# More of attention's output projection behind its last scores, the mixer's first norm five steps sooner, and the last output projection in two halves

## The chip, the core and the metric

The kernel runs on one core of one Trainium2 chip. The metric is the device time of one execution in microseconds (us); the kernel before was run three times. Its engines are TensorE (PE; its weight loads are shown apart as PEld), VectorE (DVE), ScalarE (ACT), GpSimd (POOL) and SyncE (SP), which issues the transfers (DMA). A matmul reads an operand that was loaded into the array ahead of it and writes to one of the PSUM banks.

## The reference

Two layers are applied twice in turn to x of 2048 rows by 640 columns: attention with a memory (A) and a gated mixer (B).

```
x = x + A(layernorm(x));  x = x + B(layernorm(x))
x = x + A(layernorm(x));  x = x + B(layernorm(x))

A:  q, k, v = x @ wq, x @ wk, x @ wv         # 32 heads of 20; 4 segments s of 512 rows
    for s in range(4):                       # M, z: sums over earlier segments
        p = softmax(qs @ ks.T * scale + causal_mask)
        a_mem = phi(qs) @ M / (phi(qs) @ z + 1e-6)
        o_s = g * a_mem + (1 - g) * (p @ vs)
        M = M + phi(ks).T @ vs;  z = z + sum(phi(ks))
    return concat(o_s) @ wo

B:  z = gelu(x @ w_in)                       # 640 -> 1728
    z1, z2 = z[:, :864], layernorm(z[:, 864:])
    g = w_sp @ z2 + b_sp                     # w_sp is 2048 x 2048, over the rows
    return (z1 * g) @ w_out                  # 864 -> 640
```

## The kernel before

**Products in three parts.** An f32 operand is split into a high and a low f16 part, and a product is made of three matmuls: high by high, high by low, low by high. A projection of 640 to 320 columns is thus 5 x 3 = 15 matmuls in one bank. Rows are worked in 16 tiles of 128.

**Attention** (`Attention.run`) makes one list of 64 pairs: 4 segments by 16 pairs of heads. A pair has three steps, so the steps go from t = 0 to 191, with some steps of lead ahead and a few behind in which the last pairs are finished (`END`). In each step `scores` issues matmuls of queries by keys twice over: once for a pair several steps ahead, into mp, whose row maxima VectorE takes (mx, L1289), and once for the pair of the step, into es (L1273, masks L1245), of which ScalarE makes the exponentials P (L1282). `maxes` (L1307 to L1312) turns the maxima into a row (mr) and stores it beside the queries in qk with two small transfers on SP, one for its high and one for its low part; es needs both. `cast` splits P into PH (ScalarE, L1299) and PL (L1300: GpSimd, or VectorE for the second head of the last four pairs). `pvs` multiplies them with the values vs (L1326: 20 matmuls pv for a head, each with a load of PH or PL). `combine` scales the sums (ab on VectorE, L1342), adds them on GpSimd, and for each group of heads makes a high and a low part ohl (ScalarE L1353, GpSimd L1354) and stores the two parts with two transfers (L1357) to o in DRAM.

Between these steps stand the dense jobs: the projections to queries and keys (L1107), to values (v0 to v15, L1050), and the output projection of a tile, p0 to p11 (`project`: o is loaded by a transposing transfer at L1065, x at L1074; two halves of 15 matmuls yps, L1083; VectorE adds x at L1089; x1 is stored at L1091). The output of tiles 12 to 15 is projected in the mixer instead. `order` lists the jobs, and PACE says how much of them goes with a step from each time on, in units of work:

```
U, V = 6480, 4530
PACE = (-LEAD, 2400), (0, 700), (53, 1150), (128, 1250), (END + G, 0)
```

U is the work of one unit of queries and keys, V that of one projection. TensorE's order is the order of this code; the order of the other engines' instructions and of SP's queue is decided when the kernel is built, by a scheduler that knows priorities.

**The mixer's first product** (`phase1b`) takes tile after tile: load x1 (L275) or, for tiles 12 to 15, load o by a transposing transfer (L281) and x (L278) and project them; norm (xn, on VectorE, with two small GpSimd operations); cast to a high and a low part (xnhl, ScalarE L231); transpose by a transfer (th, L233); 30 matmuls zp by the second half of the weights (wi1), then 30 by the first half (wi0), all L316; gelu on ScalarE (L322). The first tile's norm may be issued ahead of attention's end: `self.first = self.ended()`, taken in `run` at step 3N - 4 = 188 of the 192, raises the priority of the first two loads, of the first norm and of its transpose, and lets them go behind the instructions that were the last on the engines at that step.

In the first round wi0 is read from the input in five pieces of 128 x 864 (`Weight.load`, L123, into wst, of which there are two buffers); each piece is split into a high part (wi0h, ScalarE L84) and a low part (wi0l, VectorE L85). In the second round the split halves are read back from DRAM.

**The spatial product and the output** are `phase2` in the first round and `phase2s` in the second. `phase2s` works on pairs of tiles, with seven products over blocks of w_sp in five banks a to e. `gate` multiplies by z1 and makes the operand ut; `tail` is the output projection of one tile (21 matmuls in each of two halves, cyp, L506; one addition of x1 on VectorE over both halves, xo, L509; one store, L510). The last two tiles' `tail` stand at the end, behind the loop over the pairs.

Of the kernel before, what the change touches and what calls it, by code (L numbers as in the profile page):

```python
# [9 lines left out]
F32 = mybir.dt.float32  # L10
# [5 lines left out]
ALU = mybir.AluOpType  # L16
# [382 lines left out]
def phase2s(g, w_sp, x1_d, z1_d, zb, w0, out):  # L399

    nc, tc = g.nc, g.tc
    KO, NP = 7, NT // 2
    RING = 6
    kn = [128] * 6 + [FH - 768]
    ks = [0, 1, 2, 3, 6, 7, 4, 5]
    with ExitStack() as ctx:
# [3 lines left out]
        po, pt1, pt0 = pool("do", 1, side="right"), pool("dtr1", 1, side="right"), pool("dtr0", 1, side="right")  # L410
# [67 lines left out]
        def fetch(nm, t, src):  # L478
            o = p2.tile([128, src.shape[-1]], F32, tag=nm, name="c" + nm)
            nc.sync.dma_start(o, src)  # L480
            return o
# [14 lines left out]
            nc.sync.dma_start(ut.rearrange("p l k c -> p (l k) c"), hl.rearrange("p l c -> p (l c)"), transpose=True)  # L496
            return t, ut[:, 0], ut[:, 1], xs

        def tail(t, uh, ul, xs, x1=None):
            if x1 is None:  # L500
                x1 = fetch("x1", t, x1_d[t])
            yp = py.tile([128, 2, 512], F32, tag="yp", name="cyp")
            for k in range(KO):
                for j, (a, b) in enumerate(((uh, woh), (uh, wol), (ul, woh))):
                    for n in range(2):
                        nc.tensor.matmul(yp[:, n, :320], a[:kn[k], k, :], b[:kn[k], k, n * 320:(n + 1) * 320],  # L506
                                         start=(k == 0 and j == 0), stop=(k == KO - 1 and j == 2))
            xo = po.tile([128, 2, 320], F32, tag="xo", name="xo")
            nc.vector.scalar_tensor_tensor(xo, yp[:, :, :320], xs, x1.rearrange("p (n c) -> p n c", n=2), ALU.mult, ALU.add)  # L509
            return lambda: nc.sync.dma_start(out[t], xo.rearrange("p n c -> p (n c)"))  # L510
# [27 lines left out]
        woh, wol = g.wu.place(w0)  # L538
        for _ in g.wu.load(None):
            pass  # L540
        pend, sent = [], lambda: None
        for p in range(NP):
            t, last = 2 * p, p + 1 == NP
            bank = lambda nm: pg.tile([128, 512], F32, tag=nm, name="g" + nm)
            vec = lambda nm: pv.tile([128, FHH], F32, tag=nm, name=nm)
            u, u1 = [p2.tile([128, FH], F32, tag="u", name="u") for _ in range(2)]
            pa, pb, pc, pd, pe = [bank(nm) for nm in "abcde"]
            v, v1, q, q1 = [vec(nm) for nm in ("v", "v1", "q", "q1")]
            n = 7 * p
# [22 lines left out]
            if pend:  # L572
                sent = tail(*pend.pop(0))
# [12 lines left out]
            x1 = [fetch("x1", i, x1_d[i]) for i in (t + 1, t)[:2 - last]] + [None]  # L586
# [18 lines left out]
            plus(u[:, FHH:], pe, t, u[:, FHH:])  # L605
            pend.append((*gate(t, u, z1[1]), x1[1]))
            sent = lambda: None
        for x in pend:
            tail(*x)()


def phase2(g, w_sp, x1_d, z1_d, zh, zl, out, nxt):
# [242 lines left out]
class Attention:  # L855
# [365 lines left out]
    def fetch(self, n):  # L1221

        assert n - self.NQK <= self.last, (n, self.last)
        assert NU * (n // 16) + min(n % 16 // 3, NU - 1) <= self.stacked, (n, self.stacked)
        for h in range(2):
            c = 40 * (n % 16) + 20 * h
            self.last_of["SP"] = self.nc.sync.dma_start(self.qk[n % self.NQK][64 * h:64 * h + 60], self.st[n // 16 % 2][c:c + 20].rearrange("p l i c -> (p l) i c")).ins
# [133 lines left out]
    def run(self, nseg=NSEG):  # L1361
        pairs = [(s, m, h0) for s in range(nseg) for m in range(NU) for h0 in UH[m][::2]]
        N = self.N = len(pairs)
        LEAD = self.LEAD = 3 * self.LM + self.LF
        G = 48
        END = 3 * N + self.LV + 3
# [9 lines left out]


        U, V = 6480, 4530
        PACE = (-LEAD, 2400), (0, 700), (53, 1150), (128, 1250), (END + G, 0)
        order = "02 03 v4 04 v5 v6 v7 10 11 12 13 14 v8 v9 v10 v11 20 21 p0 22 23 24 v12 v13 v14 v15 30 31 p1 32 p2 33 p3 34 p4 p5 p6 p7 p8 p9 p10 p11".split()  # L1380

        def step(w):

            for (t, p), (e, _) in zip(PACE, PACE[1:]):
                if w <= p * (e - t):
# [81 lines left out]
        def until(t):  # L1467
            while streams:
                e = min(streams)
                if e[0] >= t:  # L1470
                    return
                with self.hold() if e[1] < 2 else ExitStack():
                    e[0] = next(e[2], None)
                if e[0] is None:
                    streams.remove(e)
# [2 lines left out]
            self.later[3 * i - LEAD + 8] = [lambda w=w: self.update(*w)]  # L1478
        for t in range(-LEAD, END):
            self.now = t  # L1480
            if t == 3 * N - 4:
                self.first, self.end_of = self.ended(), [*self.last_of.values()]
            f, c = divmod(t + self.LF, 3)
            if c == 0 and 0 <= f + self.LM < N:
                self.fetch(f + self.LM)
            p, r = divmod(t - self.LV - 2, 3)
            if r == 0 and 0 <= p < N:
                self.combine(p, *pairs[p])
            n, c = divmod(t, 3)
            self.scores(n, c)  # L1490
            for f in self.later.pop(t, ()):
                f()
            for h in range(2):
                p, r = divmod(t - self.LV - h, 3)
                if r == 0 and 0 <= p < N:
                    for _ in self.pvs(p, h, *pairs[p]):
                        pass
                if h == 1 and c == 0 and 0 <= n - 1 + self.LM < N:
                    self.maxes(n - 1 + self.LM)
                if r == 0 and 0 <= p + 1 < N:  # L1500
                    self.cast(p + 1, h)
            until(t + 1)
# [87 lines left out]
```

## Time and profile before

| | |
|---|---|
| median of three runs | 2333.38 us |
| the runs | 2327.29, 2333.38, 2336.17 us |
| the profiled execution | 2329.32 us |
| its span in the trace | 2327.4 us |
| mean granted TensorE clock | 0.983 |
| busy: PE, PEld | 2172.4 us (93%), 1299.1 us (56%) |
| busy: DVE, ACT, POOL | 1502.1 us (65%), 1174.6 us (50%), 974.4 us (42%) |
| chain that ended last | PE 69%, DVE 9%, ACT 7%, DMA 6%, issue 3% |

All times below are us from the start of the span. A row of the timeline has the start, the duration, the engine (SPq: a transfer's issue on SyncE), the line, the operation, output <- input and the shape; xN stands for N instructions in a row, and a bracket for the idle time ahead of them and what ended it. Durations of many instructions are busy times. PE's share is that of an engine that has something in the array, which is not the same as full speed.

### The profile page before, as it was taken

Reading aid. Unit: us, or ns where it says so; the run is one execution under the profiler, and the core shown is the slowest. Engines: PE = TensorE matmul, PEld = TensorE weight load, DVE = VectorE, ACT = ScalarE, POOL = GpSimd, SP = SyncE. Lnnn points to the kernel's source line nnn. Section 1 sums busy time; section 2 is a strip of 40 time slices with the busy share of each in tenths; the row PEclk is TensorE's granted clock in tenths of the full one; section 3 lists DMA queues with packets and bytes.
Section 4 is the critical chain, followed back from the end, with each engine's and each line's share of the span. In section 5 each row is a group of like instructions: output and inputs, shape, how many; then the busy total and the mean of one; then the engine's idle time right before and its main releaser. Section 6 shows DMA issues by size and latency. Waiting matters only on the chain.

```text
span 2327.4 us, 50389 instructions
## 1 busy us (share of the span) xinstructions
PE 2172.4 (93%) x20490; PEld 1299.1 (56%) x20490; DVE 1502.1 (65%) x2790; ACT 1174.6 (50%) x1452; POOL 974.4 (42%) x726
## 2 busy tenths in 40 slices
PE   5878889899989999999999888999997999999998
PEld 2445455656645555555555555656665555555655
DVE  7678878876664544445335788787766767546454
ACT  3369678877742332122113887887775324322221
POOL 2168678988720000000001888888875323000000
PEclk9999899999999999999999999999998999999999
DMA  5653544545463458878645336453465433977875
GB/s 162 165 139 95 129 114 124 136 142 131 128 190 101 123 172 220 225 216 216 168 134 145 75 101 168 113 130 89 121 175 149 108 102 101 263 201 192 226 206 123
DMA packets 509417, 350.16 MB, mean 150 GB/s; under 512 B 409280, under 2 KB 444224, under 8 KB 504064
## 3 DMA queue, kind: packets, MB, share of 16 engines
q1 hardware_dynamic: 509184, 346.93, 56.1%
q8 instruction: 161, 2.64, 0.5%
q14 instruction: 72, 0.59, 0.1%
HBM read 160.83 MB, written 97.93 MB: 111 GB/s over the span
## 4 chain that ended last, share of the span: by engine, by line
PE 69%; DVE 9%; ACT 7%; DMA 6%; issue 3%; POOL 2%; SPq 1%; ACTq 0%; DVEq 0%; POOLq 0%
PE zp L316 15%; PE gp L668 12%; PE cyp L700 4%; PE pv L1326 4%; PE cyp L506 4%; PE yps L1083 3%; PE kps L1107 3%; PE ga L469 3%; PE mp L1273 3%; PE qps L1107 3%; PE gb L469 3%; DVE mx L1289 3%; PE vps L1050 2%; ACT P L1282 2%; ACT PH L1299 2%
## 5 line engine op out<-in xcount | busy, mean ns | idle before, releaser
L1300 POOL TENSOR_TENSOR PL<-P,PH 128x1280 f16<-128x1280 f32 x248 | 649.8, 2622 | 168.2 <-ACT PH L1299 158.7
L1289 DVE TENSOR_REDUCE mx<-mp 128x2 f32<-128x1024 f32 (+3 forms) x512 | 409.0, 817 | 106.1 <-PE mp L1245 104.5
L1282 ACT ACTIVATE P<-es,sc 128x1024 f32<-128x1024 f32 (+1 forms) x384 | 370.7, 965 | 140.7 <-PE es L1245 138.4
L1299 ACT CAST PH<-P 128x1280 f16<-128x1280 f32 x256 | 320.5, 1253 | 21.0 <-PE pv L1326 13.5
L219 POOL TENSOR_TENSOR lnrs<-lnve,mhalf 128x1 f32<-128x1 f32 x92 | 57.0, 628 | 555.0 <-DVE lnve L218 555.0
L316 PEld LDWEIGHTS <-th 128*128 128x128 f16 x1920 | 188.6, 98 | 171.7 <-DMA th<-xnhl 8.3
L668 PE MATMUL gp<-zh,wt 128*128 128x432 f16 x1024 | 231.2, 346 | 0.0
L668 PEld LDWEIGHTS <-wt 128*128 128x128 f16 x1536 | 150.2, 98 | 129.0 <-DMA wt<-wn 0.3
L1273 PEld LDWEIGHTS <-qk 60*128 60x128 f16 (+1 forms) x2048 | 91.1, 93 | 222.3 <-issue 154.4
L469 PEld LDWEIGHTS <-wt 128*128 128x128 f16 x1344 | 131.5, 98 | 112.6
L1326 PE MATMUL pv<-vs,PH 128*128 128x41 f16 x2560 | 168.4, 183 | 5.8 <-DVE ab L1342 5.7
L1273 PE MATMUL es<-qk 64*128 64x512 f16 (+3 forms) x1024 | 134.9, 299 | 39.5 <-ACT P L1282 28.1
L1326 PE MATMUL pv<-vs,PL 128*128 128x41 f16 x2560 | 164.5, 182 | 7.6 <-POOL PL L1300 5.3
L1273 PE MATMUL mp<-qk 60*128 60x512 f16 (+3 forms) x1024 | 138.1, 307 | 34.3 <-DVE mx L1289 33.3
L1245 PEld LDWEIGHTS <-big 64*128 64x128 f16 x3072 | 140.9, 95 | 50.6 <-issue 3.7
L316 PE MATMUL zp<-wi1h,th 128*128 128x432 f16 x640 | 150.5, 350 | 7.3 <-DMA th<-xnhl 7.3
L1050 PE MATMUL vps<-wvh,xt 128*128 128x320 f16 x640 | 152.4, 303 | 4.7 <-DVE vs L1056 4.1
L1326 PEld LDWEIGHTS <-PH 128*128 128x128 f16 x2560 | 142.9, 96 | 22.0 <-ACT PH L1299 3.9
L1326 PEld LDWEIGHTS <-PL 128*128 128x128 f16 x2560 | 143.5, 97 | 10.7 <-POOL PL L1300 6.0
L668 PE MATMUL gp<-zl,wt 128*128 128x432 f16 x512 | 135.3, 346 | 0.0
L1107 PE MATMUL kps<-xt,wkh 128*128 128x512 f16 x380 | 121.4, 389 | 8.9 <-DVE phl L1141 8.8
L681 DVE TENSOR_TENSOR u<-u,cz 128x864 f32<-128x864 f32 x16 | 17.0, 1060 | 160.7 <-ACT u L679 130.1
(248 smaller groups left out, 4389.8 us busy)
## 6 DMA issues: line engine op xcount, KB each, us to landing
wr<-in_B_w_sp_dram SPq DMA_DIRECT2D x32, 1024.0 KB
qk<-st SPq DMA_DIRECT2D x256, 120.0 KB
x<-x SPq DMA_DIRECT2D x56, 320.0 KB
z<-z SPq DMA_DIRECT2D x32, 432.0 KB
cz<-z SPq DMA_DIRECT2D x32, 432.0 KB
turned<-wt SPq DMA_DIRECT2D x24, 512.0 KB
wt<-turned SPq DMA_DIRECT2D x24, 512.0 KB
st<-qhl SPq DMA_DIRECT2D x40, 256.0 KB
```

Source lines behind the costliest of these rows:

```text
L316: nc.tensor.matmul(zp[:, n, :FHH], a[:, k, :], b[:, k, c:c + FHH], start=(k == 0 and j == 0), stop=(k == KD - 1 and j == 2))
L469: nc.tensor.matmul(o[:, :FHH], wt[:, x, m, :], zb[b][:, y, m, :], start=start and i == j == 0, stop=i == NP - 1 and j == 2, skip_group_che ...
L668: nc.tensor.matmul(gp[:, n, :FHH], ready[t][:, k % 2, a, k // 2, :], b[:, k, n * FHH:(n + 1) * FHH], start=(i == 0 and j == 0), stop=(i == ...
L1050: nc.tensor.matmul(ps, a[:, k, c], b[:, k, n * 320:(n + 1) * 320], start=(i == 0), stop=(i == 14))
L1107: nc.tensor.matmul(ps, a[:, k, c], b[:, k, :], start=(i == 0), stop=(i == 14))
L1245: nc.tensor.matmul(out, g.big[r, 64 - 64 * s:192 - 64 * s], mk, start=False, stop=s == 1, skip_group_check=True)
L1273: nc.tensor.matmul(out[:, h, o:o + w], a[r, ac], b[r, bc], start=o == 0, stop=False, skip_group_check=True)
L1282: self.last_of["ACT"] = nc.scalar.activation(P[:, :, 512 * c:512 * c + ew], es[:, :, :ew], AF.Exp, scale=g.esc).ins
L1289: self.last_of["DVE"] = nc.vector.tensor_reduce(self.mx[m][:, :, i], mp[:, :, o:o + w], AX.X, ALU.max).ins
L1299: nc.scalar.copy(PH, P[:, h])
L1300: (nc.gpsimd if h == 0 or n < self.N - self.TAIL else nc.vector).tensor_tensor(PL, P[:, h], PH, ALU.subtract)
L1326: nc.tensor.matmul(pv[:, i, h, :], x[:, c:c + 128], v[:, j, h0 + h, :], start=(j == 0 and x is PH), stop=(j == i and x is PL), skip_group_ ...
```

## The change

It has three parts. First, from step 128 on a step takes 1115 units of dense work in place of 1250, so the last output projections come later. Second, `first` is taken at step 3N - 9 = 183 in place of 188. Third, in `phase2s` the very last output projection is made by a function of its own: each half of 320 columns in a bank of its own (a and b, those of the spatial products), with an addition and a store of its own.

```
+        def out_half(o, n, k, uh, ul):
+            for j, (a, b) in enumerate(((uh, woh), (uh, wol), (ul, woh))):
+                nc.tensor.matmul(o, a[:kn[k], k, :], b[:kn[k], k, n * 320:(n + 1) * 320],
+                                 start=(k == 0 and j == 0), stop=(k == KO - 1 and j == 2))
+
+        def last_tail(t, uh, ul, xs, x1):
+            x1 = fetch("x1", t, x1_d[t])
+            xo = po.tile([128, 2, 320], F32, tag="xo", name="xo")
+            for n, o in enumerate((pa, pb)):
+                for k in range(KO):
+                    out_half(o[:, :320], n, k, uh, ul)
+                c = slice(n * 320, n * 320 + 320)
+                nc.vector.scalar_tensor_tensor(xo[:, n], o[:, :320], xs, x1[:, c], ALU.mult, ALU.add)
+                nc.sync.dma_start(out[t][:, c], xo[:, n])
+
-        def tail(t, uh, ul, xs, x1=None):
-            if x1 is None:
-                x1 = fetch("x1", t, x1_d[t])
+        def tail(t, uh, ul, xs, x1):
...
-        for x in pend:
+        for x in pend[:-1]:
             tail(*x)()
+        pa, pb = bank("a"), bank("b")
+        last_tail(*pend[-1])
...
-        PACE = (-LEAD, 2400), (0, 700), (53, 1150), (128, 1250), (END + G, 0)
+        PACE = (-LEAD, 2400), (0, 700), (53, 1150), (128, 1115), (END + G, 0)
...
-            if t == 3 * N - 4:
+            if t == 3 * N - 9:
                 self.first, self.end_of = self.ended(), [*self.last_of.values()]
```

The new lines shift those behind them: L1083 (yps) is L1098 in the changed kernel, L1065 (o) L1080, L1074 (xt) L1089, L1091 (x1) L1106, L1282 (P) L1297, L1299 (PH) L1314, L1312 (mr) L1327, L1326 (pv) L1341, L1353 and L1357 (ohl) L1368 and L1372. Lines up to L498 stay.

Three places show how the instructions move. The first is on TensorE, at the end of the first round's attention. Before, the rows end the last pv group, and zp by wi1h (the high part of wi1) follows it:

```order
L1326 MATMUL pv<-vs,PH 128x41
L1326 LDWEIGHTS PL
L1326 MATMUL pv<-vs,PL 128x41
L316 LDWEIGHTS th
L316 MATMUL zp_11225<-wi1h,th 128x432
```

In the changed kernel a pv group is followed by projections (o: the attention output of a tile, woh and wol: the two parts of wo):

```order
L1341 MATMUL pv<-vs,PH 128x41
L1341 LDWEIGHTS PL
L1341 MATMUL pv<-vs,PL 128x41
L1098 LDWEIGHTS o
L1098 MATMUL yps<-woh,o 128x320
L1098 LDWEIGHTS o
L1098 MATMUL yps<-wol,o 128x320
```

Behind the scores of step 191 stood four pv groups of 20 and then zp; now stand there pv 20, yps 3, pv 20, yps 18, pv 20, yps 3, pv 20, yps 24, then zp. The second round has the same order.

The second place is on SP's queue some steps ahead of that. The names: qk_219 and qk_220 are query and key buffers that take a row of maxima, o_2 and o_3 the attention output of the third and the last segment in DRAM, x_0_n the tile n of x1 in DRAM. Before:

```order
L1312 DMA qk_219<-mr 2x4x128
L1357 DMA o_3<-ohl 128x4x120
L1312 DMA qk_219<-mr 2x4x128
L1065 DMA_TRANSPOSE o<-o_2 128x10x128
L1357 DMA o_3<-ohl 128x4x120
L1091 DMA x_0_10<-x_10705 128x640
L1312 DMA qk_220<-mr 2x4x128 x2
```

In the changed kernel:

```order
L275 DMA x_11194<-x_0_0 128x640
L275 DMA x_11207<-x_0_1 128x640
L1327 DMA qk_219<-mr 2x4x128
L1372 DMA o_3<-ohl 128x4x120 x2
L1327 DMA qk_219<-mr 2x4x128
L1106 DMA x_0_8<-x_10535 128x640
L1089 DMA xt<-in_A_x_dram 128x640
L1327 DMA qk_220<-mr 2x4x128 x2
```

The mixer's first two loads of x1 now stand ahead of these rows, the second mr stands behind both stores of ohl where it stood behind one, and x1 of tile 8 is stored where it was tile 10.

The third place is on SP's queue at the mixer's start in the first round (wst: the pieces of wi0 from the input; th: the transposed norm). Before:

```order
L123 DMA wst<-in_B_w_in_dram 128x864 x2
L1091 DMA x_0_11<-x_10859 128x640
L275 DMA x_11270<-x_0_2 128x640
L233 DMA_TRANSPOSE th<-xnhl 128x10x128
L123 DMA wst<-in_B_w_in_dram 128x864
L275 DMA x_11367<-x_0_3 128x640
L123 DMA wst<-in_B_w_in_dram 128x864
L233 DMA_TRANSPOSE th<-xnhl 128x10x128
L123 DMA wst<-in_B_w_in_dram 128x864
L1357 DMA o_3<-ohl 128x4x160 x2
```

In the changed kernel:

```order
L233 DMA_TRANSPOSE th<-xnhl 128x10x128
L1106 DMA x_0_10<-x_10903 128x640
L1372 DMA o_3<-ohl 128x4x160
L123 DMA wst<-in_B_w_in_dram 128x864 x2
L1372 DMA o_3<-ohl 128x4x160
L1106 DMA x_0_11<-x_11024 128x640
L281 DMA_TRANSPOSE o<-o_3 128x10x128
L123 DMA wst<-in_B_w_in_dram 128x864 x2
L278 DMA xt<-in_A_x_dram 128x640 x2
L123 DMA wst<-in_B_w_in_dram 128x864
```

The transpose of the first norm now stands ahead of all loads of wi0, and these stand among the last stores of ohl: two behind the first store, two behind the second store, the store of tile 11's x1 and a transpose of o_3, and the last behind two more loads.

## The prediction

> **What bounds the kernel now.** I read the page first, then the busy time of three stretches, then the waits of TensorE in the stretch where attention hands over to the mixer, and last the timeline there and at the end.
>
> ```profile
> PE 2172.4 (93%) x20490; PEld 1299.1 (56%) x20490; DVE 1502.1 (65%) x2790; ACT 1174.6 (50%) x1452; POOL 974.4 (42%) x726
> ```
>
> TensorE is busy for 93% of the span, so a change pays only where TensorE stands still, or where work is taken from it. The next rows give stretch, length, then busy time (instructions) of PE, PEld, DVE, ACT, POOL, the granted clock, DMA share and GB/s: steps 128 to 181 of the first attention round, its end with the hand-over, and the same steps of the second round.
>
> ```profile
> 477.00:618.00 141.00, 139.41 (x1958) 90.71 (x1957) 102.39 (x206) 106.23 (x127) 118.23 (x80) 1.00 0.54 147
> 618.00:650.00 32.00, 20.73 (x348) 14.32 (x347) 24.75 (x43) 22.25 (x25) 21.08 (x16) 0.90 0.45 130
> 1619.00:1755.00 136.00, 132.50 (x1862) 86.09 (x1859) 95.19 (x191) 100.42 (x120) 110.47 (x74) 0.99 0.52 143
> ```
>
> In the first stretch TensorE is idle for 1.59 of 141 us: these steps are bound by its matmuls. In the second it is idle for 11.27 of 32 us, since the four last groups of products with values (pv) stand there with nothing between them and wait. For what, this says (total, times, longest):
>
> ```profile
> PE zp L316 <- DMA th<-xnhl: 3.1, 1, 3.1
> PE es L1273 <- DMA qk<-mr: 2.6, 2, 2.0
> PE pv L1326 <- DVE ab L1342: 2.0, 1, 2.0
> PE pv L1326 <- POOL PL L1300: 1.9, 1, 1.9
> PE pv L1326 <- DVE PL L1300: 1.0, 2, 0.5
> ```
>
> The mixer's first product (zp) waits 3.1 us for its transposed norm (th), the pv groups 4.9 us for softmax parts and the sums made of earlier groups, the scores (es) 2.6 us for row maxima (mr).
>
> **Part 1: projections moved to the end (both rounds).** The first stretch holds these exponentials, one to a step, and a projection's matmuls (yps) cost this:
>
> ```profile
> L1282 ACT ACTIVATE P<-es,sc x54: 681/1092/1121, 477.0 to 615.0; 128x1024 f32<-128x1024 f32 x36, 128x512 f32<-128x512 f32 x18
> ```
> ```profile
> 607.30 2.14 PE yps L1083 x15
> ```
>
> One yps takes 2.14/15 = 0.143 us. Counted in the order of the instructions, the 54 steps hold 267 yps before and 216 now, so 51 x 0.143 = 7.3 us of TensorE work leave a stretch that TensorE bounds. Behind the last scores stood none; now 48 stand there: 24 between the pv groups, 24 behind the last. The first 24 (3.4 us) lie in the 4.9 us that the pv groups wait and cost nothing; if that wait were gone, they would cost their 3.4 us. The last 24 (3.4 us) take the place of the wait for th.
>
> What is late next in the 54 steps is GpSimd: 118.23 us of work in 141 - 7.3 = 133.7 us, 88%. So a part of the saved time returns as waits: between 0 and the whole 7.3. I take 0.9, nearer to nothing, because the waits now are 1.59 us at GpSimd's 84%. Kept: 6.4 us a round.
>
> **Part 2: first norm five steps sooner (both rounds).** It moves two loads of x1, two norms on VectorE, two casts on ScalarE, two small GpSimd operations and two transposes on SP's queue ahead of the last steps. The wait for th goes, but the 24 yps fill it, so by itself that is worth 0. VectorE's share is hidden by its idle time (32 - 24.75 = 7.25 us in the second row above); without that cover the last PL would come later, which is a rival below. The o loads that queue behind the transposes are needed only some steps later: 0.
>
> There is a gain, though, because TensorE no longer stops ahead of zp:
>
> ```profile
> 649.92 0.90 PE L316 MATMUL zp<-wi1h,th 128*128 128x432 f16 x2 [3.13 <-DMA th<-xnhl]
> ...
> 657.22 0.53 PE L316 MATMUL zp<-wi0h,th 128*128 128x432 f16 x2
> ```
> ```profile
> 732.63 10.95 PE zp L316 x60
> ```
>
> The first 30 matmuls took 657.22 - 649.92 = 7.30 us; 30 normally take 10.95/2 = 5.48. So 1.8 us a round are lost to the slow clock after the gaps, and with 24 yps ahead that is gone.
>
> The order of SP's queue costs something. The second half of a row maximum (mr) now queues behind both stores of ohl, before behind the first only (SP's row for that mr, GpSimd's for the value of the second store, and the scores that wait):
>
> ```profile
> 626.08 0.51 SPq L1312 DMA_DIRECT2D qk<-mr  x1
> ```
> ```profile
> 625.65 1.09 POOL L1354 TENSOR_TENSOR ohl<-oat,ohl 128x480 f16<-128x480 f32 x1 [0.70 <-ACT ohl L1353]
> ```
> ```profile
> 627.86 0.39 PE L1273 MATMUL es<-qk 64*128 64x512 f16 x2 [2.03 <-DMA qk<-mr]
> ```
>
> The second store can go at 625.65 + 1.09 = 626.74, takes about 0.5, and the mr goes at some 627.3 in place of 626.08: 1.2 us more, and es is already waiting for it. Behind es queue the exponentials, the casts and every later pv. Loss 1.2 us a round (0 to 1.7).
>
> A round thus gains 6.4 + 1.8 - 1.2 = 7.0 us.
>
> **Part 3: the mixer's second weight half, first round only.** Wi0 is loaded in five pieces through two buffers, and the first zp by wi0 comes 30 matmuls after th is first used. Before, the first two loads left 0.03 us after the last projection's addition (639.79 + 0.55), while attention still ran:
>
> ```profile
> 639.79 0.55 DVE L1089 SCALAR_TENSOR_TENSOR x<-yps,sc,xt 128x320 f32<-128x320 f32 x1
> ...
> 640.37 0.81 SPq L123 DMA_DIRECT2D wst<-in_B_w_in_dram  x2
> ...
> 644.48 2.05 ACT L84 ACTIVATE wi0h<-wst,iv 128x864 f16<-128x864 f32 x2 [1.85 <-DMA wst<-in_B_w_in_dram]
> ...
> 646.92 1.35 SPq L233 DMA_TRANSPOSE th<-xnhl  x1
> ...
> 650.09 0.50 DVE L1342 TENSOR_TENSOR ab<-pv,rs 128x328 f32<-128x328 f32 x1
> ...
> 652.16 1.01 ACT L84 ACTIVATE wi0h<-wst,iv 128x864 f16<-128x864 f32 x1 [1.47 <-DMA wst<-in_B_w_in_dram]
> 653.21 1.12 DVE L85 SCALAR_TENSOR_TENSOR wi0l<-wst,iv,wi0h 128x864 f16<-128x864 f32 x1 [1.40 <-ACT wi0h L84]
> 653.87 1.72 POOL L1354 TENSOR_TENSOR ohl<-oat,ohl 128x640 f16<-128x640 f32 x1 [1.68 <-ACT ohl L1353]
> 654.79 1.23 SPq L1357 DMA_DIRECT2D o<-ohl  x2
> ...
> 660.04 1.28 ACT L322 ACT_TABLE_LOAD   x1 [0.27 <-DMA o<-ohl]
> ```
>
> That addition now follows the last 24 yps. Let 0 be the end of the last pv. The yps end at 3.4, the addition at 4.0, and loads 1 and 2 leave at 4.0 and 4.4. A load lands 644.48 - 640.37 = 4.1 us after its issue, a high half takes 2.05/2 = 1.0 us on ScalarE, a low half 1.12 on VectorE. Pieces 1 and 2 are whole at 10.3 and 11.4. Load 3 now stands behind the last store of ohl and behind a transpose of what it stored (L281). The last sum (ab) is done at about 1.0, an estimate from its 0.50 and two smaller operations ahead of it. From its end (650.59) to that of the low half of ohl (653.87 + 1.72 = 655.59) passed 5.0 us, of which ScalarE spent 0.9 on a piece of wi0 (the row at 652.16); without those the store goes at 1.0 + 4.1 = 5.1. It lands 4.4 later (655.6 to 660.0, when the table load stops waiting for it), and the transpose takes 1.35 to issue by the row of another: load 3 leaves at 10.8 and piece 3 is whole at 10.8 + 4.1 + 2.1 = 17.0. Load 5 needs the buffer of piece 3: whole at 17.0 + 6.2 = 23.2.
>
> TensorE has done the 30 zp by wi1 at 3.4 + 5.5 = 8.9 and could end those by wi0 at 14.4. It ends them at 23.2 + 0.7 = 23.9 instead: a wait of 9.5 us that was not there. Could load 3 go as soon as its buffer is free, at 10.3, it would be 9.0; with the 0.9 us and a second transpose ahead of load 3 it would be 11.8. ScalarE's table load and first gelu now stand between pieces 2 and 3, in time in which it waits for load 3 anyway.
>
> This wait comes in pieces, and after such gaps the clock may be low again; I take 0.9, half of the 1.8 above (0 to 1.8). The row below at 2308.98 shows it after 2.38 us of idling: 7.54 in place of 5.87 us. The Trainium skill, in "TensorE: Matmul & The Clock Gate", Part 1: The HAM clock gate, lets TensorE fall to half its clock only after an idle window of about 3.4 us, and gives it back after as long of work. By that rule gaps this short would cost nothing, and the sum would be 0.9 us better. Here the trace disagrees with the first half (2.38 us were enough) and agrees with the second (slow from 649.92 to about 653.5, 3.6 us).
>
> In the second round wi0 lies ready long before: 0.
>
> **Part 4: the last output projection in two halves.**
>
> ```profile
> 2308.98 7.54 PE L506 MATMUL cyp<-w,ut 128*128 128x320 f16 x42 [2.38 <-DVE xo L509]
> ...
> 2317.50 5.87 PE L506 MATMUL cyp<-w,ut 128*128 128x320 f16 x42 [0.97 <-DVE xo L509]
> ...
> 2324.32 0.33 SPq L510 DMA_DIRECT2D out_dram<-xo  x1
> ```
>
> In other banks it need not wait for the addition before it: 0.97 us. Its 42 matmuls stay 42. Between their end (2323.37) and the last store lie 0.95 us, nearly all of it an addition of 640 columns; one of 320 takes 0.55 by the row of L1089, so 0.3 go. The last store is half as large; from its issue to the span's end at 2327.4 are now 3.1 us, of which between 0 and 1.5 go: I take 0.2, since its start is not shortened. The wait at 2308.98 stays. Gain 1.5 us (1.3 to 2.8).
>
> **Sum**, against the profiled execution's 2329.32 us: 2 x 7.0 - 9.5 - 0.9 + 1.5 = 5.1 us faster, 2324.2. That execution lies 4.06 us under the median of the runs (2333.38), so I give 2328.
>
> **Rivals.** *The weights arrive in time.* If loads 3 to 5 overtook what they queue behind, all but 0 to 1 us of the 10.4 would stay away: 15.5 us faster, 2313.8, or 2317.9 by the median (-0.66%). For it: TensorE waited for no piece of wi0 before. Against it: the position on the queue, and two buffers only. Chance 0.15.
>
> *The steps do not shorten.* GpSimd at 88%, with VectorE between, could pace the 54 steps. The waits would return all 7.3 us; left are 2 x (1.8 - 1.2) + 1.5 - 10.4 = 7.7 us slower, 2337.0, or 2341.1 by the median (+0.33%). It decides from 0.9 + 5.1/2 = 3.4 us of new waits a round. For it: 3.5 us of idling in the second round's stretch already. Against it: the 1.59 us of the first. Chance 0.17.
>
> *The sooner norm delays the last softmax parts.* Two casts and two norms stand ahead of the last PH and PL on ScalarE and VectorE; if the last pv comes 2 us later in each round, 1.1 us of gain are left: 2328.2, or 2332.3. For it: the pv groups wait for just these engines. Against it: VectorE's 7.25 us of idling. Chance 0.15.
>
> **How the numbers follow.** The forecast has 0.50, 0.03 are left for what I do not see. A measurement of this kernel can tell about 0.5% (11.7 us) from no change. Faster by more: the first rival and a little, 0.17. Slower by more: a third of the second rival with some of the unseen, 0.08. Within: 0.75. The range goes from the first rival's time to a little short of the second's, with the runs' spread: 2317 to 2339.
>
> **What would show it.** In the profile after: 54 exponentials in some 135 us rather than 141; no wait of zp for th; waits of zp for wi0 or its splits of about 9 us in all in the first round and none in the second; es waiting some 3.2 us for mr; the last two output projections without a gap. If zp does not wait for wi0, part 3 is wrong; if the 54 steps still take 140 us, part 1 is.

## The result, and the profile after

| kernel | median | runs | ratio to before, 95% interval |
|---|---|---|---|
| before | 2331.84 us | 20 (2327.29 to 2336.17) | |
| changed | 2324.93 us | 20 (2317.56 to 2331.88) | 0.9971 [0.9963, 0.9978] |

The change makes the kernel 0.29% faster: 6.8 us of 2331.8, with an interval of 5.1 to 8.6. It was forecast 5.1 us faster.

The profiled execution of the changed kernel is the slowest of its 20 (2331.88 us, span 2330.2), so its stages are read here, not its sum; a second profile, of the same kernel (after_again below), has a span of 2318.7. The row of busy times in the changed kernel hardly differs from before:

```profile
PE 2173.5 (93%) x20490; PEld 1297.3 (56%) x20490; DVE 1503.4 (65%) x2791; ACT 1174.3 (50%) x1452; POOL 971.5 (42%) x726
```

The work is the same, so what changed is where TensorE stands still. The 54 exponentials of steps 128 to 182 in the first round, in the profile of that slowest execution ("on record" below) and in the second one (count, shortest, median and longest in ns, first and last start):

```profile
L1297 ACT ACTIVATE P<-es,sc x54: 687/1090/1116, 476.8 to 611.0; 128x1024 f32<-128x1024 f32 x36, 128x512 f32<-128x512 f32 x18
```
```profile
L1297 ACT ACTIVATE P<-es,sc x54: 687/1090/1118, 474.8 to 606.0; 128x1024 f32<-128x1024 f32 x36, 128x512 f32<-128x512 f32 x18
```

Before they ran from 477.0 to 615.0, 138.0 us; now 134.2 and 131.2. TensorE's waits at the hand-over to the mixer in the first round (600 to 690 us of the profile on record; total, times, longest):

```profile
PE zp L316 <- ACT wi0h L84: 8.1, 2, 6.9
PE es L1288 <- DMA qk<-mr: 3.3, 2, 2.1
PE mp L1288 <- DVE mx L1304: 2.7, 1, 2.7
PE zp L316 <- DVE wi0l L85: 1.3, 3, 0.6
PE pv L1341 <- POOL PL L1315: 1.1, 1, 1.1
```

The wait of zp for th (3.1 us) is gone, and those of the pv groups fell from 4.9 to 1.4. Two new ones stand at the top: zp waits 9.4 us for pieces of wi0 (8.1 + 1.3), and mp waits 2.7 us for the row maxima mx. The first comes from the queue that the prediction followed (SP's issues, ScalarE's table load, then the zp by wi0 on TensorE):

```profile
649.38 0.81 SPq L123 DMA_DIRECT2D wst<-in_B_w_in_dram  x2
...
656.93 1.33 SPq L281 DMA_TRANSPOSE o<-o  x1
658.39 0.96 SPq L123 DMA_DIRECT2D wst<-in_B_w_in_dram  x2
...
666.01 0.33 SPq L123 DMA_DIRECT2D wst<-in_B_w_in_dram  x1
```
```profile
654.88 0.53 PE L316 MATMUL zp<-wi0h,th 128*128 128x432 f16 x2
...
664.88 0.88 PE L316 MATMUL zp<-wi0h,th 128*128 128x432 f16 x2 [6.90 <-ACT wi0h L84]
```

Load 3 stands behind L281, which waits for the store of o_3; load 5 waits for a buffer. The second new wait is on VectorE (its rows, SP's load of x1, and TensorE's row):

```profile
616.70 0.54 DVE L1104 SCALAR_TENSOR_TENSOR x<-yps,sc,xt 128x320 f32<-128x320 f32 x1
620.03 0.89 DVE L216 BATCH_NORM_STATS2 lnst<-x 128x6 f32<-128x320 f32 x2 [2.78 <-DMA x<-x]
620.83 1.27 DVE L1304 TENSOR_REDUCE mx<-mp 128x2 f32<-128x768 f32 x2
```
```profile
615.18 0.90 SPq L275 DMA_DIRECT2D x<-x  x2
```
```profile
622.16 0.28 PE L1288 MATMUL mp<-qk 60*128 60x256 f16 x2 [2.69 <-DVE mx L1304]
```

The sooner norm's first instruction reaches VectorE 2.78 us ahead of its data, which left SP at 615.18; the next row maximum is queued behind it, and TensorE needs the bank that it reads. At the end of the span the two halves stand without a gap:

```profile
2312.61 7.54 PE L519 MATMUL cyp<-w,ut 128*128 128x320 f16 x42 [2.39 <-DVE xo L522]
2319.99 3.02 PE L501 MATMUL ga<-w,ut 128*128 128x320 f16 x21
2322.85 3.02 PE L501 MATMUL gb<-w,ut 128*128 128x320 f16 x21
```

### The profile page after: what moved, and what is told of

Its sections match the earlier page's. It is cut to its first block, busy times and chain, and to the rows that moved or that the text cites. A ratio compares the mean times of both kernels' runs of the same rounds, so it can differ in the third digit from the quotient of the medians.

```text
span 2330.2 us, 50381 instructions
## 1 busy us (share of the span) xinstructions
PE 2173.5 (93%) x20490; PEld 1297.3 (56%) x20490; DVE 1503.4 (65%) x2791; ACT 1174.3 (50%) x1452; POOL 971.5 (42%) x726
## 4 chain that ended last, share of the span: by engine, by line
PE 65%; DVE 11%; DMA 8%; ACT 7%; issue 3%; SPq 1%; POOL 1%; ACTq 0%; DVEq 0%; POOLq 0%
PE zp L316 14%; PE gp L683 10%; PE pv L1341 4%; PE cyp L715 3%; PE yps L1098 3%; PE cyp L519 3%; DVE mx L1304 3%; PE ga L469 3%; PE mp L1288 3%; PE kps L1122 3%; ACT P L1297 2%; PE qps L1122 2%; PE vps L1065 2%; PE gb L469 2%; ACT PH L1314 2%
## 5 line engine op out<-in xcount | busy, mean ns | idle before, releaser
L1297 ACT ACTIVATE P<-es,sc 128x1024 f32<-128x1024 f32 (+1 forms) x384 | 370.3, 964 | 135.3 <-PE es L1260 133.2
L1314 ACT CAST PH<-P 128x1280 f16<-128x1280 f32 x256 | 320.4, 1253 | 21.6 <-PE pv L1341 12.9
L316 PEld LDWEIGHTS <-th 128*128 128x128 f16 x1920 | 188.5, 98 | 177.2 <-issue 16.4
L1341 PE MATMUL pv<-vs,PH 128*128 128x41 f16 x2560 | 168.6, 183 | 2.1 <-DVE ab L1357 2.0
L1341 PE MATMUL pv<-vs,PL 128*128 128x41 f16 x2560 | 164.4, 182 | 4.4 <-POOL PL L1315 3.9
L1065 PE MATMUL vps<-wvh,xt 128*128 128x320 f16 x640 | 151.5, 302 | 3.6 <-DVE vs L1071 3.0
L1341 PEld LDWEIGHTS <-PH 128*128 128x128 f16 x2560 | 142.9, 96 | 18.7
L1341 PEld LDWEIGHTS <-PL 128*128 128x128 f16 x2560 | 143.4, 97 | 7.8 <-POOL PL L1315 4.7
```

What stands on the lines that cost most here:

```text
L316: nc.tensor.matmul(zp[:, n, :FHH], a[:, k, :], b[:, k, c:c + FHH], start=(k == 0 and j == 0), stop=(k == KD - 1 and j == 2))
L1065: nc.tensor.matmul(ps, a[:, k, c], b[:, k, n * 320:(n + 1) * 320], start=(i == 0), stop=(i == 14))
L1297: self.last_of["ACT"] = nc.scalar.activation(P[:, :, 512 * c:512 * c + ew], es[:, :, :ew], AF.Exp, scale=g.esc).ins
L1314: nc.scalar.copy(PH, P[:, h])
L1341: nc.tensor.matmul(pv[:, i, h, :], x[:, c:c + 128], v[:, j, h0 + h, :], start=(j == 0 and x is PH), stop=(j == i and x is PL), skip_group_ ...
```

## The experiments

Four kernels ran in each of three groups, each group beside runs of the kernel before on the same chip. All ratios are to those; "us" worked out from a ratio takes 2331.8.

| kernel | ratio, 95% interval | us |
|---|---|---|
| pace_only | 0.9993 [0.9982, 1.0004] | -1.6 |
| norm_only | 0.9949 [0.9929, 0.9968] | -11.9 |
| tail_only | 0.9991 [0.9982, 0.9999] | -2.1 |
| no_norm | 0.9975 [0.9963, 0.9986] | -5.8 |
| no_pace | 0.9954 [0.9940, 0.9969] | -10.7 |
| hold_o | 0.9969 [0.9957, 0.9982] | -7.2 |
| early_x1 | 0.9973 [0.9960, 0.9985] | -6.3 |
| mem_hold | 1.0068 [1.0052, 1.0084] | +15.9 |
| after_again | 0.9969 [0.9957, 0.9981] | -7.2 |
| zp_late | 0.9978 [0.9967, 0.9990] | -5.1 |
| two_zp | 0.9949 [0.9936, 0.9962] | -11.9 |
| two_zp_nopace | 0.9990 [0.9980, 1.0001] | -2.3 |

Where the time lies in each round, in us, from the timeline of each kernel's profile (first round / second round): from the 129th exponential to the 183rd; on to the 192nd; on to the end of the last pv; on to the first zp by wi0; the 30 zp by wi0, their waits included.

| kernel | steps 128-182 | 182-191 | last pv | to zp by wi0 | zp by wi0 |
|---|---|---|---|---|---|
| before | 141.1 / 144.6 | 20.8 / 20.7 | 8.0 / 8.2 | 10.4 / 10.6 | 5.5 / 5.5 |
| after_again | 133.4 / 134.3 | 24.8 / 25.3 | 6.8 / 6.8 | 11.1 / 9.4 | 16.4 / 5.5 |
| pace_only | 133.5 / 133.4 | 22.3 / 21.8 | 8.7 / 9.1 | 11.8 / 11.3 | 16.2 / 5.5 |
| no_norm | 133.5 / 134.8 | 22.4 / 22.4 | 8.9 / 8.7 | 12.2 / 11.6 | 14.8 / 5.5 |
| norm_only | 141.1 / 144.5 | 23.0 / 22.9 | 7.6 / 7.6 | 2.1 / 2.6 | 9.7 / 5.5 |
| no_pace | 141.0 / 142.9 | 23.2 / 22.9 | 7.6 / 7.6 | 2.1 / 2.6 | 9.2 / 5.5 |
| zp_late | 141.0 / 144.8 | 22.8 / 22.9 | 7.0 / 7.0 | 6.5 / 6.5 | 6.5 / 5.5 |

**The three parts alone, and two of them.** The four kernels of the first group:

```
pace_only, against before
-        PACE = (-LEAD, 2400), (0, 700), (53, 1150), (128, 1250), (END + G, 0)
+        PACE = (-LEAD, 2400), (0, 700), (53, 1150), (128, 1115), (END + G, 0)
norm_only, against before
-            if t == 3 * N - 4:
+            if t == 3 * N - 9:
tail_only, against before (with out_half and last_tail as in the change)
-        for x in pend:
+        for x in pend[:-1]:
             tail(*x)()
+        pa, pb = bank("a"), bank("b")
+        last_tail(*pend[-1])
no_norm, against the changed kernel
-            if t == 3 * N - 9:
+            if t == 3 * N - 4:
```

> The kernel before with the first part alone: PACE at 1115 from step 128, the first norm left at step 3N - 4, the old output tail. Theory of the record: the norm's place by itself is worth nothing, so the sum without the tail stands, 2 x 7.0 - 10.4 = 3.6 us faster than before; zp by wi0 waits some 9 to 12 us for pieces of wi0 in the first round. Rival, from the trace of the changed kernel: the sooner norm makes VectorE wait 2.8 us for the load of x1 with row maxima queued behind it, which makes the last ten steps and the last pv groups 3.6 us (first round) and 2.6 us (second round) longer; without the sooner norm this goes, so 3.6 + 6.2 = 9.8 us faster. It would also show zp waiting for th for no more than 2 us a round.

> The kernel before with the second part alone: the first norm at step 3N - 9. Theory of the record: the wait of zp for th (3.1 us) and the slow clock after it (1.8 us) go in each round, the row maximum behind both stores costs 1.2 us: 2 x 3.7 = 7.4 us faster, less what the wi0 pieces then make zp wait (0 to 3 us). Rival (VectorE waits for the load of x1, some 3.1 us a round in place of 1.2): 2 x 1.8 = 3.6 us faster at most, and TensorE waits for mx by some 2.7 us near the sooner norm.

> The changed kernel with the first norm back at step 3N - 4 (first and third part). Theory of the record: as the changed kernel, 6.9 us faster than before by its runs. Rival (the sooner norm costs 3.6 and 2.6 us through VectorE's wait for the load of x1): 6.2 us better than the changed kernel, 13 us faster than before; the step from the 183rd exponential to the last pv group takes some 29 us in place of 32.3 and 31.5.

> The kernel before with the third part alone, the last output projection in two halves. Theory of the record: 1.5 us faster (1.3 to 2.8). Rival, from the trace of the changed kernel: the gap of 0.97 us ahead of the last projection is gone, but the time from the last matmul to the end of the span is not shorter (4.3 against 4.1 us), since two stores stand there: 0.9 us faster.

pace_only came out 1.6 us faster (4.2 faster to 0.9 slower): its interval holds the 3.6 of the prediction's terms and not the 9.8 of the rival. no_norm is as fast as the changed kernel within the intervals (5.8 and 6.8 us), and not 13. So beside PACE at 1115 the sooner norm is worth next to nothing, as part 2 of the prediction had it, and what it costs on VectorE is about what it gains. norm_only is the surprise: 11.9 us, where the prediction's terms gave 7.4. The table shows that the stretch from the last pv to the zp by wi0 fell from 10.4 to 2.1 us. TensorE's groups between 640 and 650 us of norm_only say why (instructions, then busy time and mean ns, idle time):

```profile
L316 PE MATMUL zp<-wi1h,th 128*128 128x432 f16 x20 | 4.7, 346 | 0.0
L316 PE MATMUL zp<-wi1l,th 128*128 128x432 f16 x10 | 2.6, 346 | 0.0
L1326 PE MATMUL pv<-vs,PH 128*128 128x41 f16 x32 | 2.0, 181 | 0.0
L1326 PE MATMUL pv<-vs,PL 128*128 128x41 f16 x33 | 1.9, 181 | 0.0
L316 PE MATMUL zp<-wi0h,th 128*128 128x432 f16 x3 | 0.9, 344 | 2.1 <-DVE ab L1342 2.1
```

All 30 zp by wi1 ran ahead of the last 39 pv, from 640.5 to 646.1, while VectorE and GpSimd still made the last parts of softmax; the pv groups have no idle time at all. In the changed kernel projections stand there instead. tail_only agrees with the predicted 1.5 us and with 0.9 (interval 0.2 to 4.2), and can't tell them apart.

**The second group**: PACE back, and three mends of what the changed kernel's profile shows.

```
no_pace, against the changed kernel
-        PACE = (-LEAD, 2400), (0, 700), (53, 1150), (128, 1115), (END + G, 0)
+        PACE = (-LEAD, 2400), (0, 700), (53, 1150), (128, 1250), (END + G, 0)
hold_o, against the changed kernel (loaded: the last load of wi0)
-                a = load(ts[i + 2])
+                with tc.issue_after(g.wi[0].loaded) if w0 is None and ts[i + 2] >= NWO else ExitStack():
+                    a = load(ts[i + 2])
early_x1, against the changed kernel
+            if t == 3 * N - 14:
+                self.loads = self.ended([*self.last_of.values()])
             if t == 3 * N - 9:
-                self.first, self.end_of = self.ended(), [*self.last_of.values()]
+                self.first = self.loads, self.ended([*self.last_of.values()])
...
-        with first:
-            a = load(ts[0])
+        with first[0]:
+            a, a1 = load(ts[0]), load(ts[1])
+        with first[1]:
             xn = attn_out(ts[0], *a)
-            a = load(ts[1])
+            a = a1
             th = xn_t(xn)
mem_hold, against hold_o
-            p2, p1, px2, px1, sp = pool("b2", 2), pool("b1", 1), pool("bx2", 2), pool("bx1", 1), pool("bs", 2)
-            pe2, pe1, wp0 = pool("be2", 2), pool("be1", 1), pool("bw0", 1)
+            p2, p1, px2, px1 = pool("b2", 2), pool("b1", 1), pool("bx2", 2), pool("bx1", 1)
+            wp0, pe1, sp, pe2 = pool("bw0", 1), pool("be1", 1), pool("bs", 2), pool("be2", 2)
```

> The changed kernel with PACE back at 1250 (second and third part). Theory of the record by its terms: 7.4 + 1.5 = 8.9 us faster than before, so about 2 us better than the changed kernel. Rival, from the run of the second part alone: with no projections behind the last scores, the first 30 zp themselves stand among the last pv groups and fill their waits, and wi0 is late by less (zp by wi0 took 9.7 in place of 17.9 us): 11.3 + 1.9 = 13 us faster than before.

> The changed kernel, with the transposing load of tile 12's o (L281) and the loads of x with it put behind all five loads of wi0 on SP's queue in the first round. If the place on the queue costs what the record says, load 3 goes when piece 1 is whole (655.4 in place of 658.4 us), load 5 some 4 us sooner than now, and zp by wi0 ends at some 668.4 in place of 672.8 us: 4.4 us better than the changed kernel. Rival: two buffers alone set the pace, and the order on the queue is worth under 1 us.

> The changed kernel, with the mixer's first two loads of x1 at step 3N - 14 and the first norm left at 3N - 9. If VectorE's wait for that load (2.8 us, with row maxima and a PL queued behind) is what lengthens the last steps, the wait of mp for mx (2.7 us in each round) goes, and the kernel is 5 us better than the changed one. Rival: the added work of the norm on VectorE and ScalarE, or the 24 projections among the pv groups, lengthen them; then nothing that can be measured.

> The changed kernel, with L281 held back as in the run above and the mixer's pools in another order in the first round, so that the buffers of wi0's pieces lie where attention is done some 15 us sooner: loads 1 and 2 can go at some 631 in place of 649.4 us. This is the record's first rival made true in part (the weights arrive in time). Pieces 1 to 3 are whole by 655 us; pieces 4 and 5 stand behind the table load on ScalarE, which waits for the store of o_3 (657), and are whole at some 661 and 662.5: zp by wi0 ends at 663 in place of 672.8 us. 9 us better than the changed kernel if the wait is the pieces' alone; about nothing if it is given back later.

no_pace is 10.7 us faster than before, and norm_only, the same without the tail, 11.9. With the sooner norm in place, a gain by PACE at 1115 is not to be seen; most likely it costs some 4 us, though the intervals of no_pace and the changed kernel overlap a little (0.9940 to 0.9969 against 0.9963 to 0.9978).

hold_o moves load 3 ahead, and zp by wi0 takes 14.6 us in its profile, 1.8 to 3.3 less than in the two of the changed kernel and not the 4.4 expected; the time can't tell it from none. Its waits for wi0 (6.0 us) are now set by two buffers and by ScalarE's table load and gelu between the pieces:

```profile
PE zp L316 <- ACT wi0h L84: 3.5, 3, 1.8
PE zp L316 <- DVE wi0l L85: 2.5, 3, 1.3
```

early_x1 took away VectorE's wait for x1, and mp no longer waits for mx. Nothing was gained. The scores (es) wait longer instead, for the row maximum mr, and steps 182 to 191 take 24.9 us (24.8 in after_again). The value of that mr is there at 616.04, but on SP it goes behind the first store of ohl (TensorE's wait, VectorE's row, SP's rows):

```profile
PE es L1289 <- DMA qk<-mr: 3.6, 1, 3.6
```
```profile
615.77 0.27 DVE L1326 SCALAR_TENSOR_TENSOR mr<-mtp,mr 8x128 f16<-8x128 f32 x1
```
```profile
617.60 0.38 SPq L1373 DMA_DIRECT2D o<-ohl  x1
618.07 0.51 SPq L1328 DMA_DIRECT2D qk<-mr  x1
```

mem_hold did what it should at its place: zp by wi0 took 9.2 us, against 16.4. But some 26 us were lost behind that: from the end of these zp to step 128 of the second round it took 972.6 us, against 946.7 in hold_o. The first load of w_sp (wr, the spatial product's operand) left at 843.51, where it left at 781.3 in hold_o: SP waited for zp, so its memory was taken until the mixer's first products ended. The spatial product's matmuls (gp) then waited for what is made of it (TensorE's wait in all, SP's wait, SP's load, TensorE's first gp after a wait):

```profile
PE gp L684 <- DMA wt<-wn: 23.8, 4, 14.9
```
```profile
SPq L649 <- PE zp L316: 9.5, 1, 9.5
```
```profile
843.51 0.33 SPq L649 DMA_DIRECT2D wr<-in_B_w_sp_dram  x1
```
```profile
858.41 0.90 PE L684 MATMUL gp<-zh,wt 128*128 128x432 f16 x2 [14.94 <-DMA wt<-wn]
```

So the prediction's rival that the weights arrive in time was made true for the most part (5.5 us would be no wait at all), and its gain was given back with interest by another transfer; this run doesn't say what the rival would be worth without that.

**The third group**: the changed kernel once more, a test of why norm_only gains, and the wait for wi0 filled with other work.

```
zp_late, against norm_only (last_pv: the last pv matmul)
-            last = z2_half(t, w_in_half(1, *th))
+            with ExitStack() if i else tc.issue_after(g.last_pv):
+                last = z2_half(t, w_in_half(1, *th))
two_zp, against hold_o
+            if w0 is None and i == 1:
+                z1_half(ts[0], w_in_half(0, *th0))
             th1 = xn_t(xn) if i + 1 < NT else None
-            z1_half(t, w_in_half(0, *th))
+            if w0 is None and i == 0:
+                th0 = th
+            else:
+                z1_half(t, w_in_half(0, *th))
two_zp_nopace, against two_zp
-        PACE = (-LEAD, 2400), (0, 700), (53, 1150), (128, 1115), (END + G, 0)
+        PACE = (-LEAD, 2400), (0, 700), (53, 1150), (128, 1250), (END + G, 0)
```

> The changed kernel itself once more, for a second profile beside the runs of this group: 6.9 us faster than before. If the profile on record (2331.9 us, the slowest of 20 runs) is no fair picture of the first round's steps 128 to 182, they take 133.4 us here, as in the four other kernels with PACE at 1115, and not 136.4.

> The second part alone, and the first tile's zp by wi1 put behind the last pv group on TensorE (in the kernel with the second part alone 25 of the 30 stand ahead of the last 40 pv and 5 among them). If that part gains because zp fills the waits among the pv groups, this gives 2 to 3 us a round back: 6 us faster than before in place of 12. If it gains because zp no longer waits for th and the clock stays up, this changes nothing that can be measured: 10 to 12 us faster than before.

> The changed kernel with L281 held back, and in the first round the second tile's 30 zp by wi1 ahead of the first tile's zp by wi0. If the wait for wi0's pieces is the whole loss, 5.5 us of it are filled with work that had to be done anyway: some 8 us better than the changed kernel, 15 us faster than before. If VectorE and ScalarE, which split the pieces, are then late with the second tile's z, under 3 us better.

> As the run above with PACE back at 1250: the second and third part, and the second tile's zp ahead of the first tile's zp by wi0. Without the third change of order this was 12.1 us faster than before; of its waits between the last pv group and the end of the first tile's zp (5.8 us in the first round) some 3 can be filled: 15 us faster than before. If PACE at 1115 is worth its 7 to 10 us a round once wi0 no longer costs, the run above is 4 us or more better than this one; if the zp fill the same idle time that the late projections fill, they are equal.

after_again repeats the result (0.9969), and its steps 128 to 182 take 133.4 us in the first round as expected.

zp_late gives the expected 6 us back: 5.1 faster than before (2.3 to 7.7) in place of 11.9 (7.5 to 16.6). With the first zp behind the last pv, the waits of the pv groups are back (4.0 us in each round, in the first thus), and the wait for the first th is not:

```profile
PE pv L1327 <- POOL PL L1301: 2.3, 1, 2.3
PE pv L1327 <- DVE ab L1343: 1.2, 1, 1.2
```

That bears out the mechanism: norm_only gains by the removed wait for th and the clock, and by the zp that fill the pv groups' waits. The medians give about half to each, but their intervals meet at 7.5 to 7.7 us. In the table, from step 191 to the end of the zp by wi0, norm_only is ahead by 3.3 us in the second round and by 0.6 in the first, where its zp by wi0 wait longer for the pieces.

two_zp is 11.9 us faster than before, 4.7 better than after_again in the same group; 8 were expected. Counted from the first zp to the mixer's last zp, its first round takes 198.7 us against 202.7. The 30 zp of the second tile fill the wait for wi0, but the zp by wi0 still idle 3.7 us in all (2.0 of them for one piece, 1.1 for ScalarE to empty the bank):

```profile
PE zp L316 <- ACT wi0h L84: 2.0, 1, 2.0
PE zp L316 <- ACT z L329: 1.1, 1, 1.1
```

two_zp_nopace lost time in a way that I had not priced. There TensorE had nothing else left when the third tile's th came late. The two buffers of th didn't hold it, since the zp by wi0 of the first tile were done at 662.23. Its cast on ScalarE (xnhl) stood behind a gelu that waited for the second tile's zp by wi0, and SP's transpose went at 675.65 (TensorE's row, then ScalarE's):

```profile
678.65 0.90 PE L316 MATMUL zp<-wi1h,th 128*128 128x432 f16 x2 [6.71 <-DMA th<-xnhl]
```
```profile
671.98 0.98 ACT L329 ACTIVATE z<-zp,sc 128x864 f32<-128x864 f32 x1 [6.30 <-PE zp L316]
...
673.66 0.72 ACT L231 CAST xnhl<-xn 128x640 f16<-128x640 f32 x1
```

So it can't say whether late projections and early zp fill the same time; no_pace and norm_only beside the changed kernel say it, as far as their intervals go. Three kernels beat the one before by some 0.5%: two_zp, norm_only and no_pace. two_zp's interval lies just under that of the changed kernel's 20 runs (0.9936 to 0.9962 against 0.9963 to 0.9978), but it overlaps that of after_again beside it (0.9957 to 0.9981).

## Why the prediction was right, and which of its steps were not

The time was right (2324.9 us, forecast 2328, range 2317 to 2339), and so were the two large terms, of opposite sign. Most terms were off, though, and that the sum came out within 2 us is in part luck: steps 128 to 182 gave more than forecast, the end of attention and the stretch behind it less. Measured values are those of after_again against before.

**Steps 128 to 182: mechanism right, term too small.** Forecast 6.4 us a round, measured 7.6 and 10.3. The waits that were to return (0.9) did not; TensorE's busy time and GpSimd's in these windows (stretch, length, busy PE, PEld, DVE, ACT, POOL, clock, DMA, GB/s), of after_again in the first and second round, then of before in the second:

```profile
474.78:608.21 133.43, 132.41 (x1909) 85.82 (x1908) 101.43 (x203) 106.39 (x128) 117.21 (x80) 1.00 0.51 140
...
1613.02:1747.30 134.28, 132.52 (x1911) 85.44 (x1911) 100.74 (x201) 106.88 (x128) 117.10 (x78) 1.00 0.53 141
```
```profile
1609.93:1754.50 144.57, 141.07 (x1960) 91.36 (x1959) 102.43 (x206) 106.35 (x128) 118.39 (x80) 0.99 0.54 144
```

GpSimd is at 117.21 / 133.43 = 88%, as forecast, and TensorE idles 1.02 us: the rival by which GpSimd paces the steps is refuted. In the second round TensorE is busy 8.6 us less (141.07 to 132.52) and idles 1.7 us less. The 51 yps at 0.143 us are 7.3 of the 8.6; for the rest there is only the granted clock, 0.99 before and 1.00 now.

**The end of attention: the step that failed.** The prediction put 24 projections among the pv groups at nothing and the sooner norm at 1.2 us, through the row maximum that queues behind two stores. From step 182 to the end of the last pv it took 2.9 and 3.1 us more: steps 182 to 191 took 4.1 and 4.5 us more, the last pv groups 1.2 and 1.5 less. The parts alone, over the same stretch: 2.3 and 1.9 us by the projections (pace_only), 1.8 and 1.5 by the norm (norm_only). The projections filled the waits of the pv groups only in part: with them alone the last pv groups take 8.7 and 9.1 us, more than before, and TensorE still waits 2.1 us for PL there; only with the sooner norm beside them do they take 6.8.

The place of the norm's cost was wrong as well. TensorE waited for mx behind VectorE's wait for x1 (2.2 and 3.0 us in after_again), and the wait for mr was about as long as before (2.1 and 2.6 us, before 2.6 and 2.4). The two stores ahead of that mr cost it nothing: on record its value was there at 623.69 (VectorE's row), and it left at 623.72 (SP's rows):

```profile
623.42 0.27 DVE L1325 SCALAR_TENSOR_TENSOR mr<-mtp,mr 8x128 f16<-8x128 f32 x1
```
```profile
619.91 1.56 SPq L1372 DMA_DIRECT2D o<-ohl  x2
623.72 0.51 SPq L1327 DMA_DIRECT2D qk<-mr  x1
```

The prediction had looked at VectorE's idle time (7.25 us) and not at the order in its queue, where an instruction that waited for a transfer held those behind it (the 2.78 us at 620.03 above). A store ahead of mr does cost something once VectorE's wait is taken away: that is early_x1, where es waited 3.6 us. Why the projections alone lengthen steps 182 to 191 (1.5 and 1.0 us) was not tried.

**Up to zp by wi0.** The slow clock after the wait for th went as forecast: the first 30 zp take 5.5 us in place of 7.3. The wait for th was filled by projections as forecast (in the first round of after_again these ran at the slow clock: 5.6 us from the last pv to zp, against 3.9 on record); no_norm shows that the sooner norm is then worth nothing by itself. Of the forecast 1.8 us a round, this stretch gave 1.3 in the second round and lost 0.6 in the first. What the prediction did not see is the norm's worth without PACE: norm_only runs the zp among the pv groups.

**The pieces of wi0: mechanism right, the wait in part by luck.** Forecast 9.5 us of waiting, measured 9.4 (on record) and 8.4. The slow clock was mis-sized: the 30 zp by wi0 took 17.9 and 16.4 us, of which 5.5 are work, so 3.0 and 2.5 us are the clock's, in place of 0.9. The loads left later than forecast: counted from the last pv, load 3 at 12.9 us on record (forecast 10.8) and load 5 at 20.5 (17.0), and the zp by wi0 ended at 27.3 (forecast 23.9, with the slow clock 24.8). The wait matches all the same, because TensorE spent part of that time at the slow clock.

**The tail: right within what can be told.** Forecast 1.5 us, timed 2.1 (0.2 to 4.2). The gap of 0.97 us is gone; the end of the last matmul lies 4.3 us ahead of the end of the span, 4.0 before.

Summed for after_again: 2.9 + 0.6 + 10.9 - 7.6 = 6.8 us slower in the first round, 10.3 - 3.1 + 1.3 = 8.5 faster in the second, and the tail's 2.1 faster. That is 3.8 us faster, against 7.2 timed; stretches that the change doesn't touch differ between two profiles by as much (start to step 128: 472 to 480 us in these kernels). What remains open is what late projections are worth once wi0 costs nothing: the one kernel that brought it nearly in time (mem_hold) lost more elsewhere.

## What to carry to other kernels

Two edits that fill the same hole are not to be priced one by one: the sooner norm alone was worth 11.9 us, more projections alone 1.6, and both with the tail 6.8. Ask of every idle stretch which of the candidates would fill it at no cost behind it; here the mixer's own products did, while the projections made the next stage's weights late. And where work is moved ahead on an engine, look at what its first instruction waits for, since all that is queued behind waits as well.

## What the runs showed of the hardware that was not expected

TensorE's clock after short gaps did not go by their length alone. After 2.39 us of idling the 42 matmuls of a projection took 7.54 us (the row at 2312.61 above; 5.87 normally). After 2.62 us of idling in norm_only the 30 zp of the second round took their normal time:

```profile
1782.54 5.65 PE L316 MATMUL zp<-w,th 128*128 128x432 f16 x30 [2.62 <-DVE ab L1342]
```

The Trainium skill, in "TensorE: Matmul & The Clock Gate", Part 1: The HAM clock gate, asks for some 3.4 us of idling before the clock halves. The second case agrees, the first (which stood in the profile before already) does not; after the 6.90 us gap at 664.88 two zp took 0.88 us in place of 0.53, as it says.

The traces show what else decides: where the gap lies. In all 14 of them the granted clock changes only at multiples of 3.41 us from its last change. Cut at these points (stretch, length, busy PE and so on; the clock is the third figure from the end), the gap of 2.38 us in before lies in one stretch, whose busy time is 1.03 us, and the clock is halved in the next; the gap in norm_only is shared by two stretches, busy for 1.92 and 2.29 us, and the clock stays:

```profile
2305.69:2309.10 3.41, 1.03 (x8) 0.61 (x7) 2.19 (x5) 1.01 (x1) 0.00 (x0) 1.00 0.04 8
2309.10:2312.52 3.42, 3.42 (x14) 1.98 (x13) 0.00 (x0) 0.00 (x0) 0.00 (x0) 0.50 0.97 230
```
```profile
1778.00:1781.41 3.41, 1.92 (x45) 1.44 (x42) 1.86 (x5) 0.98 (x1) 1.26 (x2) 1.00 0.02 5
1781.41:1784.83 3.42, 2.29 (x13) 1.28 (x14) 2.54 (x10) 0.44 (x1) 2.27 (x5) 1.00 0.00 0
1784.83:1788.24 3.41, 3.41 (x21) 1.80 (x20) 3.41 (x3) 1.84 (x5) 2.90 (x2) 1.00 0.58 161
```

Over all stretches of the 14 traces at full clock, each of the 157 in which TensorE idled for more than 55% was followed by half the clock, but only 2 of the 8630 in which it idled for less than 35%. Between these bounds it was 59 of 295, and what decides there stays open.
